# Summing and spreading the key sum z: by TensorE with a matrix of ones, or by two crossbar turns, a row sum and a repeat

## The chip, the cores and the metric

The kernel runs on one core of a Trainium2 chip. Its engines work side by side, each through its own queue in order: TensorE (PE, matmuls into PSUM), VectorE (DVE), ScalarE (ACT), GpSimd (POOL) and SyncE (SP), which here only issues transfers. Semaphores tie them together. The metric is the time of one execution on the device in microseconds (us). Before the change it is 260.26 us, the median of three runs (260.16 to 260.85).

## The reference

One input x of 2048 tokens by 640 goes through two branches, and a gate of each token mixes them. Branch A is linear attention with 32 heads of 20 columns each; branch B is a mixer with an MLP.

```python
# branch A
q, k, v = split(x @ wqkv)                    # 32 heads of 20
phi = lambda t: where(t > 0, t + 1, exp(t)) + 1e-6
pq, pk = phi(q), phi(k)
kv  = einsum("bhsd,bhse->bhde", pk, v)
z   = einsum("bhsd->bhd", pk)                # sum over all 2048 tokens
num = einsum("bhqd,bhde->bhqe", pq, kv)
den = einsum("bhqd,bhd->bhq", pq, z) + 1e-6
a   = (num / den) @ wo
# branch B
h  = gelu(layernorm(x) @ w1)                 # then four column groups, each shifted by 1 or 2 tokens
x1 = x + shift(h) @ w2
b  = x1 + gelu(layernorm(x1) @ w3) @ w4
out = g * a + (1 - g) * b                    # g = sigmoid(x . gate_w), per token
```

The change concerns z alone: a vector of 640 numbers, each the sum of one column of pk over all tokens. The denominators need it beside every token, that is, on all 128 partitions.

## The kernel before

**Tiling.** Tokens lie on partitions in 16 tiles of 128 (index t), or on the free axis in 4 chunks of 512 (index c). The 640 columns are 5 blocks of 128. The first stage makes q and k tile by tile with phi. Then GT, which is x transposed times pk, is accumulated over all tokens in five blocks (items ga and g, line 796 is the helper that emits its matmuls). kvt multiplies GT with the weights of v (line 969), Lt takes the diagonal blocks out of PSUM, and m joins them to wo. Branch B runs beside it: w1 (with a gelu on ScalarE), w2, w3 (gelu), w4. The attention rows a are made late from the normalised q and M.

**Layer norms through the crossbar.** A normalised tile xn (written by GpSimd, a ring of three buffers) is turned by a transposing transfer that SyncE issues, into xnT. The turns of the first layer norm are the items t1 0 to t1 15, of the second t2. Chunk c of w1 reads the turns t1 4c to 4c+3. The turn of a 640-column tile appears as DMA_TRANSPOSE on line 281.

**z before the change.** z_add (line 822) sums the 16 tiles of pk on VectorE, in fp32, and the last of 15 adds writes zsum in bf16: 128 partial sums on the partitions, for 640 columns. zb_group (line 1025) multiplies zsum with a matrix of ones on TensorE: that adds up the partitions, and as the stationary operand has 128 columns of ones, the result comes out on every partition at once. VectorE casts it into zb. qn_sum (line 1086) multiplies pq of a token tile with zb and reduces within the heads; qn_scale divides.

**What sets the order.** A planner written in Python (class _Items, run, lines 336 to 414) builds the queue of every engine before anything runs. Items stand in streams. An item has a duration on TensorE (zero for those that are not its main work), and dependencies with a lag. The planner keeps its own clock for each engine from a cost for each operation (line 232: for a turn, 1.35 us of SyncE's queue and 2.8 us to landing, lines 244 and 245). It picks the item with the smallest key:

```python
v = done[d] + 100.0
...
key = (max(est, t_pe), 0 if it["dur"] == 0.0 else 1, -cp[n])
```

est is the largest such v over the dependencies: an item is due 100 ns after the last of them, by the planner's clock. t_pe is TensorE's planned time, and cp the length of the chain behind the item, in which the lags count. The lags do not delay an item, they make it more urgent. All operations of an item go to their engines' queues at the moment it is picked. An operation's place in its queue is fixed by that, and on the chip each engine works its queue strictly from the front.

**The lines that matter here.** line 600 mm_group (most matmuls), 622 tensor_scalar, 630 tensor_tensor, 656 activation, 665 copy, 281 the turns, 820 the copy of a block of GT from PSUM by ScalarE, 953 kvt, 1025 zb_group, 1036 its place in the plan, 1204 the w1 items.

Of the kernel before, what the change touches and what calls it, by code (L numbers as in the profile page):

```python
# [6 lines left out]
F32 = mybir.dt.float32  # L7
ACTF = mybir.ActivationFunctionType
ALU = mybir.AluOpType

S = 2048
D = 640
# [3 lines left out]
NT = S // 128  # L16
NCH = S // 512
KD = D // 128
# [398 lines left out]
def _build(nc, A_x, A_wqkv, A_wo, B_w1, B_w2, B_w3, B_w4, gate_w, out, dbg=None, stop=None):  # L417
    sch = _Sched(nc)
# [37 lines left out]
    pa = Arena(SB_LO, SB_HI - SHARED)  # L456
# [3 lines left out]
    ps = nc.alloc_psum_tensor("ps", [128, 8, 512], F32)  # L460
# [5 lines left out]
    ones_c = pa.alloc("ones_c", [128, 768], BF16)  # L466
# [10 lines left out]
    w2 = pa.alloc("w2", [128, KD, D], BF16)  # L477
# [8 lines left out]
    M_sb = pa.alloc("M_sb", [128, KD, D], BF16)  # L486
    zb = pa.alloc("zb", [128, D], BF16)
    dnr = pa.alloc("dnr", [128, 2, 4, H], F32)
    xn = pa.alloc("xn", [128, 3, D], BF16)
    junk = pa.alloc("junk", [128, 1, D], BF16)  # L490
    qprod = pa.alloc("qprod", [128, D], F32)
    zacc = qprod
    zsum = pa.alloc("zsum", [128, D], BF16)
# [34 lines left out]
    psf = ps[:, :, :].rearrange("p b n -> p (b n)")  # L528
    bank_hold = set()

    def pair():
        best = None
        for k_ in range(4):
            q_ = (bank_rr[0] // 2 + k_) % 4
            tf = 0.0
            ok = True
            for b in (2 * q_, 2 * q_ + 1):
                if b in bank_pend or b in bank_hold:
                    ok = False
                lk = sch.locks.get(b)  # L540
                if lk is not None:
                    tf = max(tf, sch.ev_time.get((lk[1].sem, lk[1].val), 1e18))
            if ok and (best is None or tf < best[0]):
                best = (tf, 2 * q_)
        b = best[1]
        bank_rr[0] = b + 2
        bank_pend.update((b, b + 1))
        return b
# [8 lines left out]
    def nfree(ap):  # L557
        n = 1
        for d_ in ap.shape[1:]:
            n *= d_  # L560
        return n

    def in_psum(ap):
        return ap.tensor.name == ps.name

    def act(fn, reads, writes, cost=None):
        if cost is None:
            n = nfree(writes[0])
            cost = max(150.0, 100.0 + 0.833 * n + (70.0 if (reads and in_psum(reads[0])) else 0.0))
            cost += 45.0 * max(0, len(reads) - 1)  # L570
        return sch.op("act", fn, reads, writes, cost=cost)

    def dve(fn, reads, writes, cost=None):
        if cost is None:
            n = nfree(writes[0])
            cost = 65.0 + n / 0.96
        return sch.op("dve", fn, reads, writes, cost=cost)
# [7 lines left out]
    def pe(fn, reads, writes, cost=500.0):  # L585
        for w_ in writes:
            sp_, rl = sch.rects(w_)
            if sp_ == "ps":
                for (_p0, _p1, lo, hi) in rl:
                    for b in range(lo // PS_BANK, (hi - 1) // PS_BANK + 1):  # L590
                        bank_pend.discard(b)
        return sch.op("pe", fn, reads, writes, cost=cost)

    def mm_group(out_ap, pairs, reads_extra=()):
        n = len(pairs)

        def fn(e, out_ap=out_ap, pairs=pairs, n=n):
            ins = None
            for i, (l, r) in enumerate(pairs):
                ins = e.matmul(out_ap, l, r, start=(i == 0), stop=(i == n - 1))  # L600
            return ins
        reads = [a for p in pairs for a in p] + list(reads_extra)
        return pe(fn, reads, [out_ap], cost=n * (max(nfree(pairs[0][1]), 24) * 0.4167 + 2.5))
# [39 lines left out]
    def activation(out_ap, in_ap, func, scale=1.0, bias=0.0, accum=None):  # L643
        rd = [in_ap] + [a for a in (scale, bias) if not isinstance(a, (int, float))]
        wr = [out_ap] + ([accum] if accum is not None else [])
        n = nfree(out_ap)
        cost = max(150.0, 100.0 + 0.833 * n + (70.0 if in_psum(in_ap) else 0.0)) + 45.0 * (len(rd) - 1)
        if accum is not None:
            cost += 91.0
        st_ = ACT_SET.get(func)  # L650
        if st_ is not None and st_ != sch.act_func:
            cost += 1290.0
            sch.act_func = st_
        if accum is not None:
            return act(lambda e: e.activation(out_ap, in_ap, func, bias=bias, scale=scale, accum_out=accum), rd, wr, cost=cost)  # L655
        return act(lambda e: e.activation(out_ap, in_ap, func, bias=bias, scale=scale), rd, wr, cost=cost)  # L656
# [4 lines left out]
    def copy(engf, out_ap, in_ap):  # L661
        cost = None
        if engf is dve and in_ap.dtype == BF16 and out_ap.dtype == BF16:
            cost = 65.0 + nfree(out_ap) / 1.92
        return engf(lambda e: e.tensor_copy(out_ap, in_ap), [in_ap], [out_ap], cost=cost)  # L665
# [93 lines left out]
    IT = _Items()  # L759
# [262 lines left out]
        for j in range(KD):  # L1022
            sch.dma("sp", M_sb[60:68, j, :], Mt[8 * j:8 * j + 8, :], "mt", group_total=KD)

    def zb_group():
        b = pair()
        mm_group(ps[:, b, 0:512], [(ones_c[:, 0:128], zsum[:, 0:512])])
        mm_group(ps[:, b + 1, 0:128], [(ones_c[:, 0:128], zsum[:, 512:D])])
        copy(dve, zb[:, :], psf[:, 512 * b:512 * b + D])

    IT.add("KVF", ("kvt", 1), 0.0, kvt_group, deps=[(("g", KD - 1), 1.0)])
    IT.add("KVF", ("lt", 1), 0.0, lt_evac, deps=[(("kvt", 1), 0.0)])
    IT.add("KVF", ("m", 0), 0.0, m_last, deps=[(("lt", 1), 1.0), (("w1", 2, 2), 0.0)])
    IT.add("KVF", ("m", 1), 0.0, m_first, deps=[(("lt", 1), 1.0), (("w3", 0, 5), 0.0)])
    IT.add("MT", ("mt",), 0.0, m_tail, deps=[(("m", 1), 1.5), (("qt", 2), 0.0)])
    IT.add("ZB", ("zb",), 0.0, zb_group, deps=[(("z", NT - 1), 1.7), (("w2", 0), 0.0)])

    SHIFT = (1, -1, 2, -2)
    PIECES = [[(0, 128, SHIFT[j])] for j in range(4)] + [[(32 * g_, 32 * (g_ + 1), SHIFT[g_]) for g_ in range(4)]]
# [156 lines left out]
    for c in range(NCH):  # L1196
        for j in range(KD):
            deps = [(("t1", u), 0.9) for u in range(4 * c, 4 * c + 4)] if j == 0 else []
# [6 lines left out]
    for t in range(NT):  # L1205
        c = t // 4
        deps = [(("w1", c, KD - 1), GEL)]
# [8 lines left out]
    for u in range(NT):  # L1216
        deps = [(("s2", u // 4), 3.2 + 0.9 * (u % 4))]
# [8 lines left out]
    for c in range(NCH):  # L1226
        for j in range(KFF):
            deps = []
# [4 lines left out]
            if j == 0:  # L1233
                deps = deps0 + [(("t2", u), 0.9) for u in range(4 * c, 4 * c + 4)]
# [11 lines left out]
    for t in range(NT):  # L1246
        deps = [(("zb",), 1.0), (("q", max(t, 2)), 2.0)]
# [12 lines left out]
    for t in range(NT):  # L1260
        c = t // 4
        deps = [(("qt", t), 3.0), (("w4load",), 0.0), (("m", 1), 1.0), (("mt",), 2.5)]
# [29 lines left out]
def bass_gated_mix__linear_attn_block__mixer_s_mlp__prompt_kernel(  # L1292
    nc, A_x, A_wqkv, A_wo, B_x, B_w1, B_w2, B_w3, B_w4, gate_w, out
):
    assert tuple(A_x.shape) == (1, S, D) and tuple(out.shape) == (1, S, D)
    assert tuple(A_wqkv.shape) == (D, 3 * D) and tuple(A_wo.shape) == (D, D)
    assert tuple(B_w1.shape) == (D, D) and tuple(B_w2.shape) == (D, D)
    assert tuple(B_w3.shape) == (D, F) and tuple(B_w4.shape) == (F, D) and tuple(gate_w.shape) == (D,)
    _build(nc, A_x, A_wqkv, A_wo, B_w1, B_w2, B_w3, B_w4, gate_w, out)
# [28 lines left out]
```

## Time and profile before

| | before |
|---|---|
| time, median of 3 | 260.26 us |
| span of the profiled execution | 259.1 us, 4261 instructions |
| TensorE busy | 254.3 us, 98% |
| VectorE busy | 152.0 us, 59% |
| ScalarE busy | 106.6 us, 41% |
| GpSimd busy | 93.8 us, 36% |
| matmuls with zsum | 2, the first at 83.30 us |
| cast into zb | 0.82 us, at 83.77 |
| turns on SyncE's queue | 32 for xnT, 16 for pqnT, 13 for xT, 1 for GT |

Times within a profile count from the start of the span. A line of the timeline gives the start, the length, the engine, the line of the kernel, the operation, the tile written and the tile read, and a count; a bracket at its end gives the idle time of the engine ahead of it and what ended it. The end of a matmul is modelled, so successive matmuls overlap in such lines, and starts are the safer thing to compare.

### The profile page before, as it was taken

Reading aid. Unit: us, or ns where it says so; the run is one execution under the profiler, and the core shown is the slowest. Engines: PE = TensorE matmul, PEld = TensorE weight load, DVE = VectorE, ACT = ScalarE, POOL = GpSimd, SP = SyncE. Lnnn points to the kernel's source line nnn. Section 1 sums busy time; section 2 is a strip of 40 time slices with the busy share of each in tenths; the row PEclk is TensorE's granted clock in tenths of the full one; section 3 lists DMA queues with packets and bytes.
Section 4 is the critical chain, followed back from the end, with each engine's and each line's share of the span. In section 5 each row is a group of like instructions: output and inputs, shape, how many; then the busy total and the mean of one; then the engine's idle time right before and its main releaser. Section 6 shows DMA issues by size and latency. Waiting matters only on the chain.

```text
span 259.1 us, 4261 instructions
## 1 busy us (share of the span) xinstructions
PE 254.3 (98%) x1654; PEld 132.5 (51%) x1685; DVE 152.0 (59%) x288; ACT 106.6 (41%) x216; POOL 93.8 (36%) x151
## 2 busy tenths in 40 slices
PE   8999999999999999999999999999999999999996
PEld 4555555544454555554444445554455544455453
DVE  1587877899903799998997407992033410143233
ACT  1496677751365766676854240005500045100000
POOL 4013995969954029666914202320011110021001
DMA  6865998672856992552726640232000020000211
GB/s 181 246 148 137 155 226 156 186 121 50 99 109 124 355 338 47 62 101 52 105 53 122 124 66 0 47 90 67 0 3 0 3 101 0 0 3 1 104 51 51
DMA packets 51406, 25.16 MB, mean 97 GB/s; under 512 B 42766, under 2 KB 49975, under 8 KB 51386
## 3 DMA queue, kind: packets, MB, share of 16 engines
q1 hardware_dynamic: 50000, 21.47, 37.1%
q0 software_dynamic: 1136, 3.28, 5.1%
q8 instruction: 13, 0.21, 0.4%
q10 hardware_dynamic: 250, 0.14, 0.2%
q14 instruction: 7, 0.06, 0.1%
HBM read 12.05 MB, written 2.62 MB: 57 GB/s over the span
## 4 chain that ended last, share of the span: by engine, by line
PE 98%; issue 1%; DVE 1%
PE ps L600 61%; PE ps L1167 22%; PE ps L796 8%; PE ps L889 2%; PE ps L862 1%; PE ps L1079 1%; PE ps L1149 1%; PE ps L890 1%; PE ps L611 1%; DVE x_tok L639 0%; PE ps L969 0%; PE ps L998 0%; DVE xT L665 0%; PE ps L1146 0%
## 5 line engine op out<-in xcount | busy, mean ns | idle before, releaser
L600 PE MATMUL ps<-xnT,w 128*128 128x512 bf16 x348 | 80.4, 379 | 0.7 <-issue 0.2
L1167 PE MATMUL ps<-w,h2T 128*128 128x512 bf16 (+1 forms) x409 | 58.3, 298 | 0.5 <-issue 0.2
L656 ACT ACTIVATE h2T<-ps 128x512 bf16<-128x512 f32 x52 | 30.5, 598 | 67.5 <-PE ps L600 67.5
L600 PEld LDWEIGHTS ps<-xnT,w 128*128 128x128 bf16 x360 | 34.1, 98 | 38.5 <-issue 0.9
L639 DVE SCALAR_TENSOR_TENSOR x_tok<-ps,stg,abx 128x512 bf16<-128x512 f32 (+1 forms) x32 | 17.3, 550 | 61.5 <-PE ps L1167 61.5
L622 POOL TENSOR_SCALAR abx<-x_tok,stg 128x640 f32<-128x640 bf16 x16 | 15.3, 959 | 99.0 <-DVE x_tok L639 94.9
L1167 PEld LDWEIGHTS ps<-w,h2T 128*128 128x128 bf16 x416 | 32.1, 98 | 24.9 <-issue 1.1
L622 POOL TENSOR_SCALAR xn<-x_tok,st 128x640 bf16<-128x640 bf16 x32 | 35.0, 1102 | 14.4 <-DMA xnT<-xn 13.9
L656 ACT ACTIVATE Er<-ps 128x640 bf16<-128x640 f32 x32 | 22.4, 709 | 16.9 <-PE ps L600 8.4
L655 ACT ACTIVATE junk<-x_tok 128x640 bf16<-128x640 bf16 x32 | 23.6, 739 | 3.1 <-DVE x_tok L637 2.6
L656 ACT ACTIVATE hsT<-ps 128x512 bf16<-128x512 f32 (+1 forms) x32 | 18.9, 593 | 13.0 <-PE ps L600 12.7
L600 PE MATMUL ps<-M_sb,pqnT 128*128 128x128 bf16 (+1 forms) x156 | 23.6, 297 | 0.3
L600 PE MATMUL ps<-w,hsT 128*128 128x512 bf16 (+1 forms) x160 | 23.7, 299 | 0.0
L639 DVE SCALAR_TENSOR_TENSOR abx<-ps,stg,abx 128x640 f32<-128x640 f32 x16 | 14.1, 884 | 12.5 <-PE ps L600 11.5
L600 PE MATMUL ps<-wkg,xT 128*128 128x130 bf16 (+1 forms) x138 | 21.1, 298 | 0.1
L600 PE MATMUL ps<-wq,xT 128*128 128x128 bf16 (+1 forms) x128 | 19.7, 298 | 0.1
L600 PEld LDWEIGHTS ps<-w,hsT 128*128 128x128 bf16 x160 | 13.3, 98 | 12.1
L600 PEld LDWEIGHTS ps<-M_sb,pqnT 128*128 128x128 bf16 x160 | 13.2, 98 | 10.8
L796 PE MATMUL ps<-pk_tok,x_tok 128*128 128x512 bf16 x79 | 17.7, 379 | 0.1
L622 DVE TENSOR_SCALAR Er<-Er 128x640 bf16<-128x640 bf16 x32 | 11.8, 368 | 9.4 <-ACT Er L656 9.3
L637 DVE SCALAR_TENSOR_TENSOR x_tok<-ps,x_tok 128x640 bf16<-128x640 f32 x16 | 13.1, 820 | 6.8 <-PE ps L600 5.9
L1108 DVE TENSOR_TENSOR pq_tok<-pq_tok,dnr 128x300 bf16<-128x300 bf16 (+1 forms) x48 | 16.7, 401 | 0.6
(78 smaller groups left out, 228.0 us busy)
## 6 DMA issues: line engine op xcount, KB each, us to landing
w<-in_B_w_dram SPq DMA_DIRECT2D x1, 2160.0 KB, 9.3
w<-in_B_w_dram SPq DMA_DIRECT2D x1, 2080.0 KB, 14.8
out_dram<-x_tok SPq DMA_DIRECT2D x3, 640.0 KB, 3.1
x_tok<-in_A_x_dram SPq DMA_DIRECT2D x2, 640.0 KB, 5.5
w<-in_B_w_dram POOLq DMA_DIRECT2D x8, 160.0 KB, 4.5
x_tok<-in_A_x_dram SPq DMA_DIRECT2D x5, 160.0 KB, 3.0
wq<-in_A_wqkv_dram SPq DMA_DIRECT2D x5, 160.0 KB, 3.9
wkg<-in_A_wqkv_dram SPq DMA_DIRECT2D x5, 160.0 KB, 4.1
```

What stands on the lines that cost most here:

```text
L600: ins = e.matmul(out_ap, l, r, start=(i == 0), stop=(i == n - 1))
L611: ins = e.transpose(o, s_, ident[:])
L622: return engf(lambda e: e.tensor_scalar(out_ap, in_ap, s1, s2, op0, op1), rd, [out_ap], cost=cost)
L637: return dve(lambda e: e.scalar_tensor_tensor(out_ap, in0, scalar, in1, op0, op1, accum_out=accum), rd, [out_ap, accum], cost=cost + 70.0)
L639: return dve(lambda e: e.scalar_tensor_tensor(out_ap, in0, scalar, in1, op0, op1), rd, [out_ap], cost=cost)
L655: return act(lambda e: e.activation(out_ap, in_ap, func, bias=bias, scale=scale, accum_out=accum), rd, wr, cost=cost)
L656: return act(lambda e: e.activation(out_ap, in_ap, func, bias=bias, scale=scale), rd, wr, cost=cost)
L796: ins = e.matmul(o, l, r, start=(t0 + q_ == 0), stop=(t0 + q_ == NT - 1))
L862: ins = e.matmul(ps[:, b, 0:n], one[:, 0:128], one[:, 0:n], start=True, stop=True)
L889: e.matmul(ps[:, b, 0:512], l, w[:, k, 0:512], start=(k == 0), stop=(k == KD - 1))
L1108: dve(lambda e, o=o, i0=i0, i1=i1: e.tensor_tensor(o, i0, i1, ALU.mult), [i0, dnr[:, 1, sd, :]], [o], cost=cost)
L1167: ins = e.matmul(o, l, r, start=False, stop=(i == KFF - 1), skip_group_check=(n0 > 0))
```

## The change

z is summed over the partitions and spread without TensorE, in four steps that replace zb_group. z_turn sends zsum through the crossbar into zb, so that columns of z lie on partitions and the 128 partial sums along the free axis. z_rows adds them up on VectorE (a row sum of five blocks into the small tile zc, fp32) and has ScalarE write each sum 128 times along its row, into zsum's place. z_back turns that again, so that every partition holds all 640 sums in zb. It is meant to give TensorE's time back to the other matmuls and to save two PSUM banks at that place.

The items: z_turn waits for the last add of z and for t1 7; z_rows for z_turn; z_back for z_rows. The condition on the w2 tile 0 is gone.

```diff
+    zc = pa.alloc("zc", [128, KD], F32)
...
-    def zb_group():
-        b = pair()
-        mm_group(ps[:, b, 0:512], [(ones_c[:, 0:128], zsum[:, 0:512])])
-        mm_group(ps[:, b + 1, 0:128], [(ones_c[:, 0:128], zsum[:, 512:D])])
-        copy(dve, zb[:, :], psf[:, 512 * b:512 * b + D])
+    zT = zb[:, :].rearrange("p (k n) -> p k n", n=128)
+    zrep = zsum[:, :].rearrange("p (k n) -> p k n", n=128)
+
+    def z_turn():
+        sch.dma("sp", zT, zsum[:, :], "trz", transpose=True)
+
+    def z_rows():
+        dve(lambda e: e.tensor_reduce(zc[:, :], zT, mybir.AxisListType.X, ALU.add), [zT], [zc[:, :]], cost=820.0)
+        activation(zrep, zc[:, :].unsqueeze(2).to_broadcast([128, KD, 128]), ACTF.Copy)
+
+    def z_back():
+        sch.dma("sp", zT, zsum[:, :], "trz", transpose=True)
...
-    IT.add("ZB", ("zb",), 0.0, zb_group, deps=[(("z", NT - 1), 1.7), (("w2", 0), 0.0)])
+    IT.add("ZB", ("zt",), 0.0, z_turn, deps=[(("z", NT - 1), 1.7), (("t1", 7), 0.0)])
+    IT.add("ZB", ("zr",), 0.0, z_rows, deps=[(("zt",), 2.6)])
+    IT.add("ZB", ("zb",), 0.0, z_back, deps=[(("zr",), 1.5)])
```

## The prediction

> **What bounds the kernel now.** I read the page's busy shares and the chain that ended last first.
>
> ```profile
> PE 254.3 (98%) x1654; PEld 132.5 (51%) x1685; DVE 152.0 (59%) x288; ACT 106.6 (41%) x216; POOL 93.8 (36%) x151
> ...
> PE 98%; issue 1%; DVE 1%
> ```
>
> The chain is TensorE (PE) from end to end; all its recorded waits in the body of the kernel add up to well under 1 us. So work taken from TensorE is saved in full, work on other engines is free, and any wait that reaches TensorE is paid in full, because no idle time is left to absorb it.
>
> Next, the timeline of TensorE around the places that the change touches. Columns are start, length, engine and line, operation, count.
>
> ```profile
> 74.30 1.24 PE L796 MATMUL ps<-pk_tok,x_tok 128*128 128x512 bf16 x5
> 75.38 1.24 PE L600 MATMUL ps<-xnT,w 128*128 128x512 bf16 x5
> 76.55 1.13 PE L969 MATMUL ps<-GT,wv 128*64 128x60 bf16 x55
> ...
> 83.30 0.43 PE L600 MATMUL ps<-zsum,ones_c 128*128 128x512 bf16 x2
> 83.57 1.52 PE L600 MATMUL ps<-w,hsT 128*128 128x512 bf16 x10
> ```
>
> Line 83.30 is what the change removes: the next group starts 0.27 us later. Lines 74.30 to 76.55 are the place to watch: the last accumulation of GT (item g 4), the group w1 (0,4), and then the 55 small matmuls of kvt, which read GT. ScalarE (ACT) at the same place:
>
> ```profile
> 74.50 0.60 ACT L656 ACTIVATE hsT<-ps 128x512 bf16<-128x512 f32 x1 [0.48 <-PE ps L600]
> 75.58 0.60 ACT L656 ACTIVATE GT<-ps 128x512 bf16<-128x512 f32 x1 [0.48 <-PE ps L796]
> 76.65 2.44 ACT L656 ACTIVATE hsT<-ps 32x512 bf16<-32x512 f32 x4 [0.48 <-PE ps L600]
> ```
>
> The last part of GT leaves PSUM at 75.58 to 76.18, and kvt starts 0.37 us after that, right behind w1 (0,4). The slack between this copy and TensorE is thus at most some 0.3 us. Then VectorE (DVE), the SyncE queue (SP) and GpSimd (POOL):
>
> ```profile
> 70.36 1.39 DVE L630 TENSOR_TENSOR zsum<-qprod,pk_tok 128x640 bf16<-128x640 f32 x1
> 77.72 0.95 DVE L630 TENSOR_TENSOR Lt<-ps,mask 128x120 bf16<-128x120 f32 x5 [5.97 <-PE ps L969]
> ```
>
> ```profile
> 73.77 1.20 SPq L281 DMA_TRANSPOSE xnT<-xn  x1
> ```
>
> ```profile
> 76.43 0.88 POOL L622 TENSOR_SCALAR xn<-x_tok,st 128x640 bf16<-128x640 bf16 x1 [0.59 <-DMA xnT<-xn]
> ```
>
> zsum is ready at 71.75. VectorE is idle until 77.7. SyncE sends one crossbar turn after another, 1.2 us of queue each; the one at 73.77 is the tenth of the first normalisation (t1 9; two went before 57, t1 2 at 62.58). The normalise at 76.43 waited for exactly that turn (ring of three buffers), so a turn takes 2.66 us from issue to the start of its reader.
>
> [...] this trace has a 640-element f32 one at 820 ns, so I use 0.82 for the bf16 one.
>
> **The change, part by part.**
> Removed from TensorE: two matmuls, 0.27 us by the start times. With PE at 98% that is the whole direct gain: -0.27. The 0.82 us cast of zb on VectorE goes too, worth nothing, as VectorE waited there for TensorE (0.52 idle before it).
>
> Added on SyncE: two turns. Each pushes the later t1 turns back by 1.2 to 1.3. w1 chunk 2 (t1 8 to 11) starts at 86.0 on TensorE (the third w1 group from 82.22 on, by the timeline), while its last turn is issued at 76.3 and lands at 79: over 6 us to spare. Chunk 3 has more, and the w3 load at 82.95 is first read behind the second normalisation's turns, which begin at 100.15. Cost nothing.
>
> Added on VectorE: one reduce of 0.82 in an idle stretch. Cost nothing by itself.
>
> Added on ScalarE: one 640-wide copy, and this one decides. *Where do the pieces land in the queues?* The planner fixes every engine's order in advance, by its own clock. A piece with duration 0 goes out as soon as TensorE's planned time passes its due time (a dependency's end plus 100 ns, lines 390 and 395), most urgent first. I put the planner's clock on the trace by TensorE, which both run without gaps: w1 (0,0) starts at 69.98.
> The costs in the code are too kind to the other engines here. It counts 870 ns for an add of z (cost 830 plus 40), the trace shows 1385: so it has zsum at 67.8 (15 adds from 54.8), 3.9 us too early. Its nine small GpSimd operations ahead of t1 2 cost 3.3 us against 7.0 in the trace (54.03 to 61.04), so its first t1 turns are early as well: counted forward at 1.35 per turn (line 244), t1 2 is issued at 59.6 and t1 9 at 69.07.
> z_turn is due when z and t1 7 are done. t1 7 lands at 66.4 + 2.8 = 69.2, so it is first eligible at the planning step at 69.98 (the step before ends at 67.6). There the urgent t1 9 goes first, and z_turn follows: *t1 9, z_turn, t1 10*. It is planned at 70.42, landing at 73.22, due 73.32. The planning steps end at 71.06, 72.14, 73.22 and 74.30 (1.08 us per w1 group), so z_rows goes out at 74.30: after the gelu of w1 (0,3), *ahead of g 4 and of its copy of GT*. For the copy of GT to be first, the due time would have to be past 75.38, 2.1 us off; I trust the order.
>
> What the hardware then does:
> - z_turn issues behind t1 9: 73.77 + 1.20 = 75.0. zsum has been ready for 3 us.
> - It lands and releases VectorE 2.66 to 2.7 later: 77.7.
> - The reduce: 0.82, to 78.5. Some 0.1 for the hand-over: 78.6.
> - The copy on ScalarE occupies it for 0.63 until the next starts (a 640-wide one elsewhere in this trace lasts 0.73 and its follower starts 0.63 after its start): 79.2. Between the gelu that ends at 75.10 and 78.6 ScalarE stands still.
> - The copy of GT: 0.60, to 79.8 instead of 76.18.
> - kvt: 0.1 later, 79.9 instead of 76.55.
>
> TensorE waits 3.35 us. Behind kvt in its queue are w1 (1,0) and all the rest, and nothing overtakes. The gelus of w1 (0,4), 2.4 us in four pieces behind GT, end at about 82.2; the first w2 tile, which reads them, comes after kvt and three groups at 79.9 + 1.2 + 3.2 = 84.3, so no second wait. z_back is issued behind t1 14 at some 82.5 and lands at 85.1; the old zb was ready at 84.6 with TensorE 3 us further on, so the q normalisation has more room than before.
>
> Sum: 260.26 - 0.27 + 3.35 = 263.3.
> Bounds of the unknown: the landing is 2.6 at least and 4.8 at most over these turns; [...] z_turn one turn earlier or later moves everything by 1.3. The small terms give 262.7 to 263.8, one turn earlier 262.0, one later 264.6.
>
> **Rivals.**
> 1. *The clock falls as well.* The gap from the last matmul of w1 (0,4) at 76.46 to 79.9 is 3.4 us[...]: 265.0. [...]
> 2. *No wait reaches TensorE* (GT's copy stays ahead, or the turn is quick): 260.26 - 0.27 = 260.0, no change that counts, and not slower. For: zsum is ready early, every other addition falls on idle engines. Against: the order above, and ScalarE's slack of 0.3 us against a chain of 5 us (turn, reduce, copy).
> 3. *Half a wait*: z_turn goes earlier in the queue by one or two places, 260.7 to 262.0, say 261.5.
> 4. *Faster*: the shorter TensorE stream and the two PSUM banks freed remove small stalls too. 259.4 would need 0.6 us of stalls that this timeline doesn't show.
>
> **How the numbers follow.** A single wait of about 3.3 us: 0.65. With the clock falling: 0.15. No wait: 0.09. Half a wait: 0.08. Faster: 0.03. The likeliest gives 263.3. The range runs from 262.5 (the low end of the small terms, and a little for other shifts of the plan) to 265.2 (rival 1); rivals 2 to 4 stay outside. Slower by over 0.3% (above 261.04) collects the first two and nearly all of half a wait: 0.87; within 0.3%: 0.09; faster: 0.04.
>
> **What would show it.** On TensorE, a gap of about 3.3 us ahead of kvt and none elsewhere; on ScalarE, an idle stretch from 75.1 to 78.6 that ends with the 640-wide copy, and the copy of GT behind it at 79.2; on SyncE, the turn of zsum at 75.0, between t1 9 and t1 10. After that all TensorE groups late by the same amount, less 0.27 from 87 on. Matmuls of 512 columns at double spacing after the gap would be rival 1. The prediction is wrong if the copy of GT comes before the copy of z on ScalarE, or if z's turn stands elsewhere in the queue.

## The result and the profile after

The changed kernel takes 264.54 us (median of 6 runs, 263.37 to 264.89) against 260.59 us for the kernel before (6 runs): a ratio of 1.0147, with a 95% interval of 1.0123 to 1.017. It is slower by 3.95 us. Here and below, times are medians; the ratio and its interval are formed over all the runs, so the ratio can differ a little from the quotient of the two medians. Each experiment has the runs of the kernel before that were taken beside it, so that time differs a little too (260.49 to 260.66).

First the page's busy shares, the clock row of its slices and the engines' shares of the chain that ended last.

```profile
PE 257.0 (98%) x1683; PEld 132.8 (50%) x1683; DVE 151.8 (58%) x288; ACT 107.3 (41%) x217; POOL 93.4 (35%) x151
...
PEclk9999999999997999999999999999999999999999
...
PE 86%; POOL 6%; DMA 4%; SPq 1%; ACT 1%; DVE 1%; issue 0%
```

TensorE shows 2.7 us more busy time, though it does two matmuls less. That sum is no measure of the loss: 31 matmul records are missing in the trace of before (1654 matmuls against 1685 weight loads), so its busy time there is too low. The clock row has a 7 in the slice from 78.9 to 85.5 us. And the chain is no longer TensorE alone: it leaves TensorE through a DMA, ScalarE, VectorE and GpSimd. So at one place TensorE waited for the others. The timeline of TensorE says where:

```profile
70.04 4.48 PE L601 MATMUL ps<-xnT,w 128*128 128x512 bf16 x20
74.36 1.24 PE L797 MATMUL ps<-pk_tok,x_tok 128*128 128x512 bf16 x5
75.44 1.24 PE L601 MATMUL ps<-xnT,w 128*128 128x512 bf16 x5
79.36 1.78 PE L970 MATMUL ps<-GT,wv 128*64 128x60 bf16 x55 [2.69 <-ACT GT L657]
81.08 4.16 PE L601 MATMUL ps<-xnT,w 128*128 128x512 bf16 x15
85.07 1.52 PE L601 MATMUL ps<-w,hsT 128*128 128x512 bf16 x10
```

The kernel before, at the start of the w1 stream and at the first w2 tile:

```profile
69.98 4.48 PE L600 MATMUL ps<-xnT,w 128*128 128x512 bf16 x19
...
80.86 1.52 PE L600 MATMUL ps<-w,hsT 128*128 128x512 bf16 x10
```

kvt (line 970 now) starts at 79.36 instead of 76.55, and the bracket names the copy of GT as what it waited for. The three w1 groups behind it take 4.0 us to the start of the next group instead of 3.2 (in the kernel before from 77.68, where kvt ends by its line, to 80.86). Now the queues that feed this point, ScalarE, VectorE and SyncE:

```profile
74.56 0.60 ACT L657 ACTIVATE hsT<-ps 128x512 bf16<-128x512 f32 x1 [0.48 <-PE ps L601]
78.00 0.73 ACT L657 ACTIVATE zsum<-zc 128x640 bf16<-128x640 f32 x1 [2.85 <-DVE zc L1033]
78.64 0.58 ACT L657 ACTIVATE GT<-ps 128x512 bf16<-128x512 f32 x1
```

```profile
77.14 0.82 DVE L1033 TENSOR_REDUCE zc<-zb 128x5 f32<-128x640 bf16 x1 [5.35 <-DMA zb<-zsum]
```

```profile
74.40 1.28 SPq L281 DMA_TRANSPOSE zb<-zsum  x1
```

Read from the bottom up: the turn of z is issued at 74.40, directly behind t1 9, and releases VectorE 2.74 us later; the row sum takes 0.82; ScalarE, idle since 75.16, copies z at 78.00; the copy of GT, whose input has been complete since about 75.6, gets its turn at 78.64.

The second part of the loss is the clock. Busy time in windows of 1 us, with the granted clock behind the engines' columns:

```profile
78.00:79.00 1.00, 0.00 (x0) 0.00 (x0) 0.00 (x0) 1.00 (x2) 0.55 (x1) 1.00 0.72 143
79.00:80.00 1.00, 0.64 (x25) 0.67 (x26) 0.00 (x0) 0.97 (x3) 0.57 (x2) 0.60 0.49 97
80.00:81.00 1.00, 1.00 (x40) 1.00 (x34) 0.00 (x0) 0.95 (x3) 0.63 (x1) 0.50 0.47 92
81.00:82.00 1.00, 1.00 (x6) 0.39 (x5) 0.79 (x5) 0.53 (x1) 0.88 (x1) 0.50 0.80 160
82.00:83.00 1.00, 1.00 (x5) 0.39 (x4) 0.13 (x1) 0.00 (x0) 0.00 (x0) 0.69 0.74 149
83.00:84.00 1.00, 1.00 (x7) 0.41 (x6) 0.00 (x0) 0.60 (x1) 0.00 (x0) 1.00 0.47 96
```

The clock is half from 79.2 (0.60 in that window is 0.2 at full and 0.8 at half) to 82.6: 3.4 us. The matmuls of 512 columns behind kvt start 0.40 to 0.43 us apart up to 82.33, and 0.22 apart from 82.69 on.

The account, from the starts of the same groups in both traces: the w1 stream begins 0.06 later (70.04 against 69.98). kvt is late by 2.81, so 2.75 belongs to the wait. The first w2 tile is late by 4.21 (85.07 against 80.86), so the half clock cost 1.40. From there on it is a constant shift, less the two matmuls: the last sums on VectorE start 3.94 later. The two lines are from the changed kernel and from the kernel before:

```profile
260.27 1.08 DVE L640 SCALAR_TENSOR_TENSOR x_tok<-ps,stg,abx 128x512 bf16<-128x512 f32 x2 [1.92 <-PE ps L1177]
```

```profile
256.33 1.08 DVE L639 SCALAR_TENSOR_TENSOR x_tok<-ps,stg,abx 128x512 bf16<-128x512 f32 x2 [1.92 <-PE ps L1167]
```

0.06 + 2.75 + 1.40 - 0.27 = 3.94, and the medians differ by 3.95.

### The profile page after: what moved, and what is told of

Same layout as the page of the kernel before. It is cut to its first block, busy times and chain, and to the rows that moved or that the text cites. A ratio compares the mean times of both kernels' runs of the same rounds, so it can differ in the third digit from the quotient of the medians.

```text
span 263.0 us, 4289 instructions
## 1 busy us (share of the span) xinstructions
PE 257.0 (98%) x1683; PEld 132.8 (50%) x1683; DVE 151.8 (58%) x288; ACT 107.3 (41%) x217; POOL 93.4 (35%) x151
## 4 chain that ended last, share of the span: by engine, by line
PE 86%; POOL 6%; DMA 4%; SPq 1%; ACT 1%; DVE 1%; issue 0%
PE ps L601 58%; PE ps L1177 21%; POOL xn L623 3%; DMA wq<-in_A_wqkv_dram 2%; POOL st L631 2%; DMA xnT<-xn 1%; PE ps L890 1%; PE ps L797 1%; SPq L285 1%; DMA zb<-zsum 1%; PE ps L1089 1%; PE ps L1159 1%; PE ps L970 1%; DVE x_tok L640 0%; PE ps L999 0%
## 5 line engine op out<-in xcount | busy, mean ns | idle before, releaser
L601 PE MATMUL ps<-xnT,w 128*128 128x512 bf16 x360 | 82.2, 382 | 0.0
L601 PE MATMUL ps<-M_sb,pqnT 128*128 128x512 bf16 (+1 forms) x160 | 24.3, 299 | 0.0
L601 PE MATMUL ps<-wq,xT 128*128 128x512 bf16 (+1 forms) x130 | 19.8, 299 | 0.0
L1118 DVE TENSOR_TENSOR pq_tok<-pq_tok,dnr 128x300 bf16<-128x300 bf16 (+1 forms) x48 | 15.7, 381 | 0.6
```

What stands on the lines that cost most here:

```text
L1118: dve(lambda e, o=o, i0=i0, i1=i1: e.tensor_tensor(o, i0, i1, ALU.mult), [i0, dnr[:, 1, sd, :]], [o], cost=cost)
```

## The experiments

Theory A is that of the prediction with its first rival: the copy of z stands ahead of the copy of GT in ScalarE's queue, kvt waits, and in the gap the clock falls. Theory B: the two turns themselves cost, through SyncE's queue. Theory C: the half clock has nothing to do with the gap.

**The turns alone.** The kernel before with two turns of zsum into a tile without a reader; the first is behind t1 9 as in the changed kernel, the second behind t1 15 (in the changed kernel just ahead of it).

```diff
+    IT.add("ZX", ("zxt",), 0.0, zx_turn, deps=[(("z", NT - 1), 1.7), (("t1", 7), 0.0)])
+    IT.add("ZX", ("zxb",), 0.0, zx_turn, deps=[(("zxt",), 4.1), (("kvt", 1), 0.0)])
```

> The kernel before, with the two turns of zsum added at the same places of SyncE's queue (into a tile that nobody reads), z still made by TensorE. Theory A: the later turns of the first normalisation move back by 1.3 and 2.6 us and nothing waits for them: the time of before, 260.6, within 0.3. Theory B: it carries most of the loss, 262 to 264.5.

Measured: 260.49 against 260.66, ratio 0.9995 (0.9986 to 1.0005). The turns cost nothing that can be measured. Theory B falls.

**ScalarE delayed, nothing else.** The kernel before, with z still on TensorE, and one added ScalarE copy ahead of the copy of GT, in three lengths (1920, 4096 and 6400 columns; they take 1.79, 3.61 and 5.53 us, which lie on one line of 0.83 ns a column and 0.19 us besides).

```diff
+            if i == KD - 1:
...
+                act(lambda e: e.activation(wf, xf, ACTF.Copy), [xf], [wf], cost=0.0)
             activation(GT[:, i, 0:512], ps[:, b, :], ACTF.Copy)
```

> The kernel before, z untouched, with one added ScalarE copy of 4096 columns (x into w3's place ahead of its load; 0.19 + 4096 x 0.83 ns = 3.6 us) right ahead of the copy of GT of g 4. Theory A: the copy of GT starts at about 78.6 and kvt at about 79.4, a wait of 2.8 us as in the changed kernel, and the clock falls in most runs: 260.6 + 2.8 + 1.4 = 264.8 (263.4 in runs where the clock holds). Theory B: no turn was added, so the time of before, 260.6.

> The same with 1920 columns (1.79 us): the copy of GT starts at about 76.85, kvt at about 77.6. Theory A: a wait of about 1.0 us. If the clock falls only in gaps near 3 us: 261.6 and clock 1.000. If any gap can make it fall: up to 263.

> The same with 6400 columns (5.5 us): the copy of GT starts at about 80.5, kvt at about 81.3, a wait of 4.7 us. Theory A: the clock falls in every run and stays down longer after the gap or begins within it: 260.6 + 4.7 + 1.4 to 1.7 = 266.7 to 267.0.

The start of kvt in the three, shortest delay first:

```profile
77.54 1.11 PE L973 MATMUL ps<-GT,wv 128*64 128x60 bf16 x55 [0.80 <-ACT GT L656]
```

```profile
79.34 1.11 PE L973 MATMUL ps<-GT,wv 128*64 128x60 bf16 x55 [2.61 <-ACT GT L656]
```

```profile
81.12 1.78 PE L973 MATMUL ps<-GT,wv 128*64 128x60 bf16 x55 [4.53 <-ACT GT L656]
```

| added copy | idle ahead of kvt | time | before | ratio (95%) | runs with the clock below 1.000 |
|---|---|---|---|---|---|
| 1.79 us | 0.80 us | 261.76 | 260.49 | 1.0051 (1.0033 to 1.007) | 0 of 4 |
| 3.61 us | 2.61 us | 265.75 | 260.49 | 1.0195 (1.0168 to 1.0222) | 3 of 4 |
| 5.53 us | 4.53 us | 268.34 | 260.49 | 1.0305 (1.0282 to 1.0327) | 4 of 4 |

kvt starts where the sum of durations puts it (77.6, 79.4 and 81.3 were expected). A delay of ScalarE alone, without any part of the change, thus makes the wait and the fall of the clock. The middle one is the changed kernel's gap almost to the tenth. It came out 0.9 above its expectation, and the longest 1.3: in both, some 0.5 us is lost again around the first m step (the shift against before grows from 4.44 to 4.93 and from 6.98 to 7.47), and about as much once more later. At both places the trace shows TensorE waiting 0.4 us for a sum of w2 on VectorE; the shortest has one such wait, also of 0.4. Why VectorE is late there was not followed up. In the middle one the half clock costs 1.7 us: the first w2 tile is late by 4.45, of which 0.11 is the later start of the w1 stream and 2.68 the wait. In the longest it lasts 6.8 us (79.6 to 86.4), twice as long as in the changed kernel, though only some 5.3 of them fall on work.

**The gap filled.** The changed kernel with ten extra matmuls on constants ahead of kvt.

```diff
+        for _ in range(10):
+            ins = e.matmul(ps[:, b, 0:512], one[:, 0:128], one[:, 0:512], start=True, stop=True)
...
         pe(fn, [wvf[:, :], GT[:, :, :]], [ps[:, b, 0:360]], cost=1000.0)
```

> The changed kernel with ten extra matmuls of 512 columns on constant ones (2.16 us) on TensorE ahead of kvt, into the bank that kvt then overwrites; nothing else moves. Theory A with the clock as its second part: kvt still starts at about 79.4, because ScalarE is as late as before, but the idle gap is down from 2.7 to about 0.6 us, the clock stays up, and the 1.4 us of half rate vanish: about 263.1. Theory C (the half rate has another cause than the gap, or the gap costs all): no change, 264.5. If kvt's wait were not the cause, 2.2 us of added work would come on top: 266.7.

Measured: 263.44 against 260.66, ratio 1.0096 (1.0073 to 1.0118); the clock is 1.000 in all four runs.

```profile
77.35 2.35 PE L977 MATMUL ps<-const-bfloat16-1.0 128*128 128x512 bf16 x10
80.30 1.11 PE L970 MATMUL ps<-GT,wv 128*64 128x60 bf16 x55 [0.60 <-ACT GT L657]
81.56 3.19 PE L601 MATMUL ps<-xnT,w 128*128 128x512 bf16 x14 [0.16 <-issue]
```

(In this execution everything up to here is 0.8 us later than in the changed kernel's.) More work on TensorE made the kernel faster by about 1 us: the wait is as long, only no longer idle, and the groups behind kvt run at full speed again: from this line, in which the record of the first of 15 matmuls is missing, it is 3.0 us to the first w2 tile, as in the kernel before. So the 1.4 us of half clock do come from the gap, and theory C falls. What remains, 2.8 above before, is the wait of 2.75 less 0.27, to within the spread of these runs (262.99 to 263.99).

**Repair 1: the copy behind GT.** z_rows is planned after g 4.

```diff
-    IT.add("ZB", ("zr",), 0.0, z_rows, deps=[(("zt",), 2.6)])
+    IT.add("ZB", ("zr",), 0.0, z_rows, deps=[(("zt",), 2.6), (("g", KD - 1), 0.0)])
```

> The changed kernel with one more condition: z_rows is planned only once g 4 is done, so its copy stands behind the copy of GT (and the four gelus of w1 (0,4)) on ScalarE. No work is changed or moved to another engine. Theory A: no gap ahead of kvt, no slow stretch, about 260.3 where before has 260.6 (the 0.27 us of the two matmuls less). Theory B or a cost of the added ScalarE work itself: 264 or so.

Measured: 265.75 against 260.66, ratio 1.0181 (1.0147 to 1.0215), no better than the changed kernel. Here I was wrong. The gap ahead of kvt is gone, as expected, but there are others. In three of the six runs the clock fell as well (266.45 to 266.84); the trace is from one of the three in which it did not (264.12 to 265.04), so the waits alone cost this much. TensorE and VectorE of this run:

```profile
90.06 1.52 PE L601 MATMUL ps<-w,hsT 128*128 128x512 bf16 x10 [0.54 <-DVE dnr L623]
...
95.21 0.46 PE L999 MATMUL ps<-wo_aug,Lt 60*64 60x512 bf16 x6 [1.19 <-ACT hsT L657]
97.58 1.04 PE L601 MATMUL ps<-xnT,w 128*128 128x512 bf16 x4 [1.91 <-DVE x_tok L638]
```

```profile
87.49 0.83 DVE L631 TENSOR_TENSOR qprod<-pq_tok,zb 128x640 f32<-128x640 bf16 x1 [4.13 <-DMA zb<-zsum]
...
89.09 0.81 DVE L638 SCALAR_TENSOR_TENSOR x_tok<-ps,x_tok 128x640 bf16<-128x640 f32 x1
```

VectorE stands 4.13 us at the first product with zb, because zb lands only at 87.49: z_back went out behind t1 15, at 84.08. In VectorE's queue the sum of w2 1 is behind that product. Its matmuls were done by 84.8, its sum starts at 89.09 (85.13 in the kernel before). From there VectorE is behind by 4 us, PSUM banks are taken longer, and TensorE waits 0.54, 1.19 and 1.91 us (the second by way of ScalarE, whose statistics of a tile wait 1.86 us for VectorE's sum, with a gelu behind them). In the changed kernel zb lands at about 85.0, earlier than here but a little later than in the kernel before, and nothing waits for it: TensorE is 4 us later there, and with it the sum of w2 ahead of the product, which starts at 87.38.

**Repair 2: the repeat on VectorE.** z_back is held behind kvt here as well.

```diff
-        activation(zrep, zc[:, :].unsqueeze(2).to_broadcast([128, KD, 128]), ACTF.Copy)
+        copy(dve, zrep, zc[:, :].unsqueeze(2).to_broadcast([128, KD, 128]))
...
-    IT.add("ZB", ("zb",), 0.0, z_back, deps=[(("zr",), 1.5)])
+    IT.add("ZB", ("zb",), 0.0, z_back, deps=[(("zr",), 1.5), (("kvt", 1), 0.0)])
```

> The changed kernel, but the repeat of z along the row runs on VectorE instead of ScalarE (and z_back is planned behind kvt, where the changed kernel had it anyway). Theory A (kvt waits for the copy of GT, which stands behind the copy of z on ScalarE, and the clock falls in that gap): both the gap of 2.7 us and the slow stretch vanish, GT is copied at about 75.6 again, kvt starts at about 76.6, and only the two removed matmuls remain: 0.27 us under the kernel before, about 260.3 where before has 260.6. Theory B (the two turns hold up SyncE's queue and with it the normalised tiles or the weights): the time stays at about 264.5, since the turns are where they were.

Measured: 267.01 against 260.66, ratio 1.0232 (1.0213 to 1.025). Same failure: kvt on time at 76.54, the product with zb at 87.62 after a wait of 4.38, nearly the same waits on TensorE (0.78, 1.19 and 1.91 us, and one of 0.22), and the clock fell in all four runs.

To tell whether the lateness of zb is the cause, two more kernels change only where the first product with zb (qs 0) and z_back stand.

**Repair 1 with qs 0 behind w2 2**, z_back as late as before:

```diff
         deps = [(("zb",), 1.0), (("q", max(t, 2)), 2.0)]
+        if t == 0:
+            deps.append((("w2", 2), 0.0))
```

> The kernel of the run before last on this point (copy of z behind the copy of GT on ScalarE, which gave 265.8), with one condition more: qs 0 is planned behind w2 2. z_back stays as late as it was, landing at about 87.5. Widened theory A: VectorE has no sum of w2 waiting behind a product that waits for zb, the waits of 0.5, 1.2 and 1.9 us on TensorE between 89 and 98 vanish, about 260.4 (up to 261 if w2 3 still waits a little). If those waits came from something else, the order on ScalarE say: 264 to 266.

Measured: 261.04 against 260.49, ratio 1.0009 (0.9999 to 1.0019). VectorE of this kernel:

```profile
88.61 0.82 DVE L638 SCALAR_TENSOR_TENSOR x_tok<-ps,x_tok 128x640 bf16<-128x640 f32 x1 [2.68 <-PE ps L601]
...
89.36 0.82 DVE L631 TENSOR_TENSOR qprod<-pq_tok,zb 128x640 f32<-128x640 bf16 x1
```

zb lands as late as in repair 1 (3.7 us after 83.98), but the first product with it now stands behind the sum of w2 2 and waits for nothing. The three waits are gone, and with them nearly all of the loss. By the medians the kernel is still 0.55 above before; the trace shows waits of 0.20 and 0.3 us on TensorE that the kernel before does not have.

**Repair 2 without the hold on z_back, and qs 0 behind w2 1**, where the kernel before has it:

> The changed kernel with the repeat on VectorE, and the first product with zb (qs 0) planned behind w2 1, where the kernel before has it; z_back is left where the planner puts it, ahead of t1 13. Theory A, widened by what the two repairs so far showed (a product with zb that is planned before zb has landed holds the w2 sums behind it on VectorE, their PSUM banks stay taken and TensorE waits): zb lands at about 83 and is first read at about 86, so neither wait is left: about 0.27 us under the kernel before, 260.3 to 260.4 where before has 260.6. If the two turns or the VectorE work cost something of themselves, 261 or more.

Measured: 260.36 against 260.49, ratio 0.9992 (0.9984 to 1.0), clock 1.000 in all 22 runs. VectorE and SyncE of this kernel:

```profile
77.31 0.82 DVE L1033 TENSOR_REDUCE zc<-zb 128x5 f32<-128x640 bf16 x1 [5.52 <-DMA zb<-zsum]
78.17 0.82 DVE L666 CAST zsum<-zc 128x640 bf16<-128x640 f32 x1
...
85.66 0.82 DVE L631 TENSOR_TENSOR qprod<-pq_tok,zb 128x640 f32<-128x640 bf16 x1
```

```profile
79.86 1.28 SPq L281 DMA_TRANSPOSE zb<-zsum  x1
```

TensorE waits for no piece of z, nor for anything behind one. On VectorE, Lt stands behind the sum and the repeat of z and starts at 78.90 instead of 77.72, which costs nothing here. This is the change as it was meant: z without TensorE, at no cost. What it gains, 0.13 us by the medians where 0.27 were removed, lies at the edge of what can be measured; in the trace the 0.27 is there (the w1 stream starts 0.05 later than in the kernel before, the last sums on VectorE 0.22 earlier).

**The most there was to gain.** The kernel before with the two matmuls left out (zb is a copy of the partial sums, so the sum over the partitions is not taken):

```diff
-        mm_group(ps[:, b, 0:512], [(ones_c[:, 0:128], zsum[:, 0:512])])
-        mm_group(ps[:, b + 1, 0:128], [(ones_c[:, 0:128], zsum[:, 512:D])])
-        copy(dve, zb[:, :], psf[:, 512 * b:512 * b + D])
+        copy(dve, zb[:, :], zsum[:, :])
```

> The kernel before with the two matmuls of z left out: zb is copied from zsum, so the sum over the 128 partitions is not taken and the denominators are partial sums. It bounds what the change could bring at all. Expected: 0.27 us under before, 260.3 where before has 260.6; more only if the two PSUM banks had held something up.

Measured: 260.51 against 260.49, ratio 1.0003 (0.9989 to 1.0018). 0.27 us is 0.1%, which this interval does not separate from nothing; a prize of more than some 0.3 us behind the two banks is excluded by it.

**The planner told the truth about z.** As the cost of a z add was the planner's largest error here, one kernel corrects only that, to the measured 1385 ns.

> The changed kernel with the planner's cost of one add of z at 1385 ns, as measured, instead of 830; nothing else. The planner then places z_turn behind t1 15, z_rows behind w2 0 and z_back behind the loads of w3 and w4. Theory A: kvt starts on time (76.6) and nothing is slow there; but SyncE's queue is held by the w4 load until about 91, so zb lands at 93 to 95, VectorE's queue stands at qs 0 with sums of w2 behind it, and TensorE waits there instead, 2 to 5 us: 262 to 266. If a true cost of z were all that was wrong: 260.3.

Measured: 272.35 against 260.49, ratio 1.0437 (1.0412 to 1.0462), the slowest of all and beyond the expected range.

```profile
92.52 2.15 SPq L281 DMA_TRANSPOSE zb<-zsum  x1
```

```profile
100.27 0.82 DVE L631 TENSOR_TENSOR qprod<-pq_tok,zb 128x640 f32<-128x640 bf16 x1 [10.31 <-DMA zb<-zsum]
```

```profile
102.79 0.75 PE L1000 MATMUL ps<-wo_aug,Lt 60*64 60x512 bf16 x6 [7.71 <-issue]
```

kvt has no wait ahead of it, as theory A has it. But z_back now stands behind the loads of w3 and w4 on SyncE, is issued at 92.52, and then needs 7.7 us to land instead of 2.7; 4 MB of weights are landing beside it. VectorE stands for 10.3 us, TensorE for 7.7. (The bracket names no releaser for TensorE; it starts 0.1 us after the sum of w2 that stood behind the product on VectorE.) In this gap the clock falls too, in all four runs: the mean clock of 0.981 over the span of 271.6 us makes 10.3 us at half, or three stretches of 3.4. By the starts of the matmuls the last ends at about 108.7 (the ten from 108.24 take 2.42 us to the next group, 2.16 in the kernel before); in one piece, they begin at about 98.5. By the starts of the groups, against repair 2 with qs 0 later, which has no wait, this gap costs 7.8 us, a wait of 0.94 ahead of it 1.1 and the half clock 2.9: 11.8 of the 12.0 by which the medians differ. I had counted the queue, and neither the slow landing nor the clock.

## Why the prediction held, step by step

**The number.** 264.54 lies within the range, because the range reached up to the rival in which the clock falls; the likeliest case, 263.3, did not come about. That it came within 1.3 us of the time is in part luck: its wait was 0.6 too long and 1.4 of half clock was missing, so that these two errors partly cancel; the kernel before, taken again beside it, was 0.3 slower too.

**The order of the queues.** Right in every place: z's turn between t1 9 and t1 10, the copy of z ahead of the copy of GT on ScalarE, z_back between t1 14 and t1 15. The size of the loss hung on this: on ScalarE the copy of GT, whose input is complete at about 75.6, starts at 78.64 behind the copy of z, and on TensorE the w1 group behind kvt starts at 81.08 instead of 77.68.

**The wait.** 3.35 predicted, 2.75 measured. The parts fit: 2.74 from issue to release (2.66 to 2.7), 0.82 for the sum (820 ns in the kernel before for an f32 row sum of 640, 821 here for the bf16 one), 0.64 for the copy of z (0.63), 0.58 for GT (0.60). What was too long is the first term: t1 9 was issued at 73.16, not at 73.77, and z's turn at 74.40, not 75.0. Nothing in the change comes before it; the time of this turn differs between executions. Counted from the start of the w1 stream, z's turn is issued 4.4 us later here and 4.5 to 5.0 us later in the five traces of repairs and of the filled gap that have it at this place, so the wait would differ by as much.

**The clock.** This is the step that failed. The likeliest case was a single wait without it, at 263.3, and the fall of the clock had a chance of 0.15. It fell in five of the six runs. The one run without it took 263.37, close to the likeliest case; the five others took 264.28 to 264.89. That a gap of this length would mostly leave the clock alone, no trace had shown: the longest wait of TensorE in the trace of before is 0.8 us. The runs show gaps of 2.6 to 2.7 us (2.69 and 2.61, each from one trace of its kernel) with which the clock fell in 8 of 10 runs, so the measurement decides against it. What makes it fall in one run and not in another of the same kernel stays open. Its size, 1.7 in the prediction (265.0 less 263.3, not shown by a trace either) and 1.40 measured, was about right; the half clock lasted 3.4 us.

**What was costed at nothing.** The turns: right, by a run of their own. That TensorE's later groups wait for nothing more: right for this kernel, in which the first gap makes the room. In the two repairs that take the gap away and bring zb in later as well (at 87.5), its lateness costs 3.6 to 4.1 us of waits; how much of this the earlier landing of 85.0 would have cost was not run. The prediction saw that zb lands at 85.1 against 84.6 before and relied on TensorE being later; it did not say that a repair would lose that cover.

**The gain.** -0.27 from the two matmuls is in the trace (the shift falls from 4.21 to 3.94), but a kernel that has it and no wait is only 0.13 below the kernel before in the medians (repair 2 with qs 0 later).

## What to carry to other kernels

In a kernel whose one engine is full and whose queues are fixed in advance, a step moved to an idle engine is not free if it waits there (here ScalarE stood idle for 2.85 us ahead of the copy of z, and TensorE for 2.69 ahead of kvt): what counts is which instruction stands behind it in that queue, and whether the full engine needs that one. Plan the step from its slowest input, check each queue that it enters (here ScalarE, VectorE and SyncE, each of which held something up in one of these kernels), and when a wait has been taken away, look for the next one that it had covered. In these kernels a gap on TensorE of 2.6 to 2.7 us mostly cost another 1.4 to 1.7 us through the clock, half as much again.

## What the runs showed that I had not expected

In these traces the half clock came in stretches of 3.4 us: one in the changed kernel (79.2 to 82.6) and in the run with the 2.61 us gap (80.7 to 84.1), two in a row with the gap of 4.53 us (79.6 to 86.4), and some 10.3 us, three times that, with the gap of 7.71 (about 98.5 to 108.7). Where it starts varies with respect to the gap: 0.2 us before the end of it in one, 1.3 us behind it in the other. Gaps of 0.6 and 0.8 us never did it (0 of 8 runs). But no single gap has to be long: repair 1, with waits of 0.54, 1.19 and 1.91 us between 89 and 98, had the half clock in 3 of 6 runs, and repair 2, with nearly the same waits, in 4 of 4.

A turn of 128 x 640 from SBUF to SBUF took 2.6 to 2.7 us from issue to landing among other turns, 3.4 us where the load of the weights followed it directly (repair 1), and 7.7 us beside that load, with a longer hold of SyncE's queue too (2.21 and 2.15 us instead of 1.28).
